# A transformer block on one core: one load moved to another queue, six more filling products, and all engine orders replaced

## The chip, the cores and the metric

The kernel runs on one core of a Trainium2 chip. The core has five engines that work side by side and meet only through semaphores: PE (TensorE, matrix products into PSUM), DVE (VectorE), ACT (ScalarE), POOL (GpSimd) and SP (SyncE, which here only issues transfers). In the profile PEld is PE's loading of weights. Each engine executes its own instructions strictly in the order in which the program lists them. Transfers are issued on SP's or ACT's queue and carried out by 16 DMA engines. The metric is the device time of one execution in microseconds (us); less is better. Three runs of the kernel before took 280.1, 280.29 and 282.09 us, so the median is 280.29 us.

## The reference

The input x has 2048 rows (tokens) of 448 columns, in bf16. A vector c gives six rows of 448 values, which shift, scale and gate the two halves of the block:

```
mod = silu(c) @ w_mod            # sa, ca, ga, sb, cb, gb
h = layernorm(x) * (1 + ca) + sa
x = x + ga * attention(h)        # 16 heads of 28, causal, window of 256 tokens
h = layernorm(x) * (1 + cb) + sb
x = x + gb * gmlp(h)
```

The attention makes q, k and v with one matrix (448 x 1344), takes a softmax over the last 256 tokens, and ends with a 448 x 448 matrix. The gMLP makes z = gelu(h @ w_in) of 1792 columns. It splits z into z1 and z2 of 896 columns each, normalises z2, mixes it over all tokens with w_sp (2048 x 2048) plus a bias per token, and multiplies the result with z1. Last comes w_out (896 x 448). The output has the shape of x.

## The kernel before, in words

The tokens lie on 16 tiles of 128, in four blocks of four tiles. The function builds a list of operations first (`sc.add`, with the helpers `pe`, `dve`, `act`, `pool`, `turn`, `load`). Each operation knows what it needs, which engines could execute it, and which buffers it takes. Nothing is planned in the program itself: `order()` reads the text `PLAN` at the top of the file. A word of it is a letter for the engine (p PE, a ACT, d DVE, t POOL, s SP), the number of the operation in the order of its creation, and, behind dots, the buffers it gets. The order of the words of one letter is the order of that engine's instructions. So `PLAN` sets three things: on which engine an operation runs, in which order each engine works, and which buffer (a PSUM bank, for instance) each operation gets. `waits()` then puts in the semaphore waits.

The work goes through these stages.

- **Head.** x's first block arrives in two pairs of tiles (`load_x0`, L410), w_mod's first part (`wmodA`) and the weights of k and q (`wq_st`, L406) in two halves each, one half on SP's queue and one on ACT's. After that SP loads the rest of x, the weights of v, and the rest of w_mod. DVE takes the statistics of x's tiles (L631, L634), POOL the reciprocal root (L638), DVE writes the normalised tile (`xn`, L649). PE computes the modulation from c (L548), transposes the tiles (L745), and ACT or DVE writes the modulated transposed tile (`hT`, L754 and L756). The weights of k and q are copied into a padded layout (`WQK`, L620 on DVE or POOL, L621 on ACT), in four pieces each. Then come the products for the keys (L826) and the queries (L802) of the first block.
- **Filling products.** `warm(n, ...)` (L567 to L571) adds n products of a constant with itself (L514), whose result nobody reads: 27 before the modulation's products and 4 behind them.
- **Attention.** For each of the 16 tiles there are score products (L931 for the first two tiles, L961 and L972 for the others), exponentials on ACT (L917, into `PW` and `PT`), masks on DVE (L980, L1001), and products with v (L1008). DVE divides by the sum (`rec_all` L1022, `o_sb` L1024), SP transposes the result (L467), PE multiplies with the output matrix (L1034), and DVE adds it to x (L1038). Between these, the projections of the later blocks (L768, L826, L846) are evacuated from PSUM on ACT (L777, L838, L850) or DVE (L778, L839, L851).
- **Second norm and gMLP.** Statistics, normalised tile and a transpose on SP again (L467, one for each tile), modulation (L1059, L1057), then products with w_in (L1128 for z2, L1149 for z1), gelu on ACT (L1135, L1157), and the normalisation of z2 (L1140).
- **Spatial products.** 28 groups of 16 products (L1173) mix z2 over the tokens. Their right operand is w_sp transposed, which SP brings from memory with transposing transfers: 16 for the first half (`wspA`), 16 for the second (`wspB`). The very first spatial group needs all normalised z2 and all 16 wspA. DVE adds the bias (L1177), POOL multiplies with z1 (L1180).
- **Output.** Groups of products with w_out (L1192), a sum with x on DVE (`fin`, L1202, four buffers), and a store on SP (L1207).

The order of the first loads on the two queues is written in the program too, as a constraint on the planner:

```
    for row in (t_x0[:1] + t_wmA[1:] + t_x0[1:] + t_wk[1:] + t_wq[1:], [t_c] + t_wmA[:1] + t_wk[:1] + t_wq[:1]):
        for first, then in zip(row, row[1:]):
            then.after = [first]
```

The first row is SP's queue: x's first pair, w_mod's second half, x's second pair, w_k's second half, w_q's second half. The second is ACT's: c, w_mod's first half, w_k's first half, w_q's first half.

Of the kernel before, what the change touches and what calls it, by code (L numbers as in the profile page):

```python
# [12 lines left out]
d22 p44.0 s2 t25 s4 a1 p45.0 p46.0 p47.0 p48.0 p49.0 s9 s6 s8 s11 t0 d103 p50.0 p51.0 p52.0 p35.0 t26 t27 a3  # L13
p53.0 p54.0 p55.0 p56.0 d104 p57.0 p58.0 p59.0 p60.0 p61.0 p62.0 p63.0 p64.0 t30 p65.0 p66.0 p67.0 t31 t28 a5
t29 s10 a7 a36 d21 a37 d101 d102 t105 t106 p68.0 p69.0 p70.0 t32 d108.0 d107.1 p40.0 p41.1 p42 d75 t93 p43 d94
p117.2 d76 d109 p71.1 p72.1 p73.1 t96 d111 a118 p74.1 p120.3 a121 p132.1 s12 d97 a119 d112 t95 a99 d110 t113
t114 d122 p133 a134 p141.3 p142 d100 a143 d98 p129.2 p130 a131 d115.0 d116.1 p123.1 a124 p138.0 d171 d173 d169
d175 d174 d172 p365.0 a366.0 d176 d170 t177 t178 p126.6 d127 t33 p139 p135.7 p136 d125 d128 p166.6 d179.0 s14
t23 s186 p156.1 d140 t34 d240 d184 p371.0 d236 a372.1 d182 p150.0 p157 t180 t181.1 d367 d234 s187 d235 p167
d241 d168 a158 p390.0 a391.2 a392 p147.1 p148 t185.2 s189 d373 p151 p144.6 p145 p397.0 t183.3 d237 d137 d149  # L20
p153.7 p163.1 a398.3 a399 d77 d152 t78 d369 p164 p79.0 d146 a165 s188 p80 d39 a162 p418.0 a419.4.0 t191 d238
d82 p83.1 p84 d375 d239 d81 p86.0 p87 p368.0 p370 d159 d400 p374 p376 d193 d192 p426.0 d85 p154 a190 p194.1
p195 d88 a427.1 p197.0 p198 p446.0 a196 t242 d402 s13 p210.1 p211 d299 s839 t243 a199 t247 d393 d244.0 d245
t24 d377 d378.0 p203.0 p204 a447.0.1 p394.0 p454.0 a205 d395 p396 p401 t249 d428 s19 p200.0 d305 s15 d212 a155
d423 p201 d429 p403 d202 a455.5 t250.1 a160 p225.1 p226 a227 p474.0 a475.3.2 p213.0 p214 p216.1 s17 d422 d161
d456 d404 d405.1 p420.0 a421 t246.2 t91 p217 d215 p424.0 p482.0 d218 p425 d301 a38 d208 d207 p222.0 p223 d206
a483.2 d451 p430 t248.3 p431 d432 d209 a224 p231.1 p232 a233 p448.0 a449 p501.0 p219.0 d450 a502.1.0 d90 s251
d433.2 p228.1 s252 s254 p229 p220 p452.0 p476.0 s253 d221 t255 p453 p458 s841 s18 a256 d457 d484 a477 a230
t258 p509.0 t257 a510.0 p259.0 d303 p260 p459 p268.1 s843 a261 d506 p269 p503.0 s406 p529.0 p265.0 p266 d478
d300 a504 a530.5.1 p531.0 d270 p275.1 p276 d304 t92 d306 d479 p537.0 a267 d460 d302 t307 a532 t308 a538.4 d505  # L30
d461.1 d309.0 s379 s462 d310 p262.0 p480.0 t311.1 p481 d485 p263 a264 d277 p281.1 d534 p486 p487 d511 d533
a271 p557.0 s316 p282 t312 a558.2.2 p278.0 p279 d488 s434 d489.0 s490 p507.0 p508 p513 a280 d539 p565.0 p290.0
p291 d512 p514 d273 d283 t314 d315.2 d540 d515 d516.2 s319 t89 p407.1 p408 a566.1 p559.0 p585.0 p535.0 p536
p541 d292 s317 a560 t313.3 p380.0 p381 d562 d409 d410 a586.0.0 p542 p593.0 d382 d561 p435.1 p436 p463.0 p464
d383 d437 a272 a274 p587.0 p284.1 a594.4 p285 d589 p612.0 d384 t385 a588 a286 p614.0 s517 d543 d544.0 p563.0
p287.1 p288 p564 a613.5.1 d567 p569 p620.0 a289 d465 p491.0 p492 s318 d595 t321 d568 a615 p570 p293.1 p294
d616 t323 a621.2 d493 p640.0 p518.0 p519 a295 d571 d596 t322 d572.2 d590 p591.0 a641.1.2 d520 s20 d320 d438
s545 d494 d439 p642.0 t386 p546.1 p547 p592 a643 p648.0 p597 p598 t440 t441 p330.0 d548 p670.0 d549 d495
p327.1 p328 p331 d387.0 a649.0 a329 d622 d599 d600.0 p668.0 s846 a669.4.0 p340.1 d332 p341 a342 d411 t412 t413
s573 p324.0 p325 a326 t414 p618.0 d617 p619 p624 p676.0 a677.5 t388 d442 d651 d623 p625 d466 d550 p346.1 p347  # L40
d672 a348 p333.0 p334 t443.1 p696.0 d467 d626 p574.1 d627.2 p575 d673 d551 a335 a697.2.1 t444 d645 s445 t415.2
t416 p352.0 p353 a354 d644 p646.0 s417 t468 t469 t470 p704.0 a705.3 d337 d650 p647 p652 d521 s601 d576 p349.0
p350 a671 s628 a351 d338 p296.1 p653 p297 p723.0 d700 p343.0 p344 d471.1 a298 s389 p355.1 d496 d678 d654 d336
d655.0 p674.0 d339 p675 a724.0.2 p698.0 p731.0 d679 t472 s473 p356 d706 t497 a345 a699 p602.0 p603 p680 d727
p725.0 p681 d577 a357 p358.1 p359 t814 a732.4 d707 d522 p751.0 t552 s656 d701 d682 d683.2 d604 d733 t523
p702.0 p703 s16 s684 a360 t524 d817 p629.0 a752.5.0 d734 p630 d631 s844 d498.2 t499 d578 p708 p709 d710 d711.0
p759.0 p657.1 d728 s845 d756 d579 p361.0 d755 a726 p658 a760.3 s712 p753.0 p729.0 p362 d762 p779.0 t553 p730
p735 a754 p736 a363 p781.0 d761 p685.0 p686 a780.2.1 d737 d738.2 p787.0 d659 d783 p757.0 p758 d784 p763 p764
d765 d766.0 p713.1 p714 d715 t815 a788.4 d789 d790 s500 t816 p863.0 p864.1 d687 p865 d688 a782 p785.0 p786
p791 p792 s739 t580 d660 t581 t525 t526.1 t527 s528 p740.1 d793 d794.2 p741 p866 p881.2 a867 d742 p882.3 p883  # L50
p884 d605 d606 t582.0 t583 a885 p1007.0 p1008.2 p1009 a892 t554.2 a874 t555 t607 t608 d661 s556 s584 d818
p1010 t821 t820 d819 p917.3 p918.1 p919 p920 t662 t663 d689 s767 a1011 a1013 a1014 p899.2 a921 s364 d869
p768.0 p769 d743 d744 t745 a1012 d609.0 d610 a928 d632 d633 t634 s795 p796.1 p797 p900.0 p901 p1015.1 p902
d664 d716 d717 s611 a903 d665.2 t635 p1016.2 p1017 p1018 d690 d636 a910 d886 t718 a1022 d666 t691 t692 t719
t693.1 t694 s834 d894 d770 d771 d772 d798 s667 d799 p1023.3 p1024.0 p1025 d875 s695 t637.0 p1026 t638 d876
d877 s639 s857 d868 d870 d800 d801 t746 t747 a1021 a1020 t748.2 d749 t802 t803 d887 a822 d893 s750 d720.1 t721
d825 t804.0 d888 t824 s832 a1019 d823 p935.2 p936.1 p937 p938 a1029 d773 t805 a1030 d912 d930 a1027 s722 d923
a1028 a939 t774 s806 p1039.0 p1040.3 p1041 t775 p953.2 a946 p954.1 p955 a1043 t878 t879 d889 t890 d922 d895
d905 d776.2 d777 s778 t896 d924 t871 t872 a827 d929 d931 a1044 d904 d941 s838 p956 p1042 s836 d947 a964 a957
t897 a1046 d940 t925 t926 d932 t811 t828 a1045 d948 t829 d826 p1031.0 d891 p971.1 p972.2 p973 p974 d949 p989.3  # L60
a975 d911 p990.1 p991 p992 a982 a993 p1032.2 a1000 d873 d913 p1047.3 p1033 p1034 a1037 d942 p1048.1 p1049
# [191 lines left out]
def bass_adaLN_cond__sliding_block__mixer_gmlp__prompt_kernel(  # L253
# [143 lines left out]
    t_c = load("d_c", "act", 0.01, lambda e: e.dma_start(c_row[127:128, :], c[0:1, :]), prio=-98.97, land=2.5)  # L397
# [15 lines left out]
    t_x0 = [load_x0(0, "sp", -98.99, 3.55)]  # L413
# [861 lines left out]
```

## Time and profile before

| what | value |
|---|---|
| median of three runs | 280.29 us (280.1 to 282.09) |
| time of the profiled execution | 282.43 us |
| its span, first to last instruction | 280.3 us |
| PE busy | 267.8 us (96%) |
| DVE busy | 166.6 us (59%) |
| ACT busy | 124.0 us (44%) |
| POOL busy | 124.5 us (44%) |
| instructions | 8415 |

The shares are means over stages of different kinds: ACT has no work after the first 160 us, and before that it is nearly full in the attention. Rows of the timeline have the start in us, the time in us, the engine, the line of the program, the operation, what it writes and from what, and how many instructions were merged; in brackets stands the idle time before the first of them and what ended it. A queue's own rows (SPq, ACTq) show how long the issue took, not when the data landed. Rows of groups have the shape, the count, busy us and mean ns of one, then the idle time before them.

### The profile page before, as it was taken

What the parts mean: (1) busy time and instruction counts of PE and PEld (TensorE: products, weight loads), DVE (VectorE), ACT (ScalarE), POOL (GpSimd) and SP (SyncE); (2) the same over time, 40 slices, a digit from 0 to 9 for tenths busy, and PEclk for the clock granted to TensorE, in tenths of its full rate; (3) what the DMA queues carried; (4) which work ended last, traced back from release to release, by engine and by line L of the source; (5) the groups of instructions that cost most, each with busy time, mean ns of one, the idle gap of its engine ahead of it and who ended that gap; (6) DMA issues with size and microseconds to landing.
All of it is one profiled execution on the core that took longest, in us unless ns stands there. A gap on an engine that the chain in (4) does not pass through costs nothing.

```text
span 280.3 us, 8415 instructions
## 1 busy us (share of the span) xinstructions
PE 267.8 (96%) x3736; PEld 154.3 (55%) x3746; DVE 166.6 (59%) x378; ACT 124.0 (44%) x144; POOL 124.5 (44%) x179
## 2 busy tenths in 40 slices
PE   7799988999999998999999699999999999999995
PEld 5777666676777675544444244444444545444452
DVE  3789899899899899959999301100300502224143
ACT  3479998989988997375876500000000000000000
POOL 7473445360646558383956203611454621036320
PEclk9899999999999999999999999999999999999999
DMA  7997798155604655485699999100000000100013
GB/s 217 302 228 114 176 110 170 22 61 86 103 5 60 124 115 81 95 190 77 138 146 173 181 191 194 16 0 0 0 2 0 6 2 27 49 0 2 0 66 115
DMA packets 66821, 25.54 MB, mean 91 GB/s; under 512 B 58465, under 2 KB 65698, under 8 KB 66786
## 3 DMA queue, kind: packets, MB, share of 16 engines
q1 hardware_dynamic: 66064, 24.21, 46.1%
q10 hardware_dynamic: 722, 0.80, 1.0%
q8 instruction: 29, 0.48, 0.8%
q14 instruction: 6, 0.05, 0.1%
HBM read 9.01 MB, written 1.84 MB: 39 GB/s over the span
## 4 chain that ended last, share of the span: by engine, by line
PE 74%; DVE 12%; ACT 6%; DMA 3%; issue 2%; POOL 1%; SPq 0%; DVEq 0%
PE ps L1173 34%; PE ps L1128 8%; PE ps L1149 8%; PE ps L1192 6%; ACT PW L917 5%; DVE PT L980 5%; PE ps L1008 4%; PE ps L1034 3%; DMA wq_st<-in_A_wqkv_dram 3%; PE ps L961 3%; PE ps L826 2%; PE ps L768 2%; PE ps L802 2%; PE ps L846 2%; DVE o_sb L1024 2%
## 5 line engine op out<-in xcount | busy, mean ns | idle before, releaser
L1180 POOL TENSOR_TENSOR z1T<-tmpg,z1T 128x512 bf16<-128x512 bf16 x28 | 31.9, 1154 | 75.9 <-DVE tmpg L1177 75.8
L917 ACT ACTIVATE PW<-ps 128x2048 bf16<-128x2048 f32 (+1 forms) x42 | 60.0, 1451 | 5.5 <-PE ps L961 4.0
L1177 DVE TENSOR_TENSOR tmpg<-ps,bsp_bc 128x512 bf16<-128x512 f32 x28 | 19.0, 689 | 72.8 <-PE ps L1173 67.3
L1173 PE MATMUL ps<-wspA,z 128*128 128x512 bf16 x220 | 48.9, 379 | 2.5 <-issue 2.3
L1173 PE MATMUL ps<-wspB,z 128*128 128x512 bf16 x218 | 49.2, 379 | 0.3
L980 DVE TENSOR_TENSOR PT<-PW,mask 128x1024 bf16<-128x1024 bf16 x56 | 38.9, 718 | 0.6 <-ACT PW L917 0.4
L1173 PEld LDWEIGHTS ps<-wspA,z 128*128 128x128 bf16 x224 | 21.8, 98 | 28.7 <-issue 2.6
L1173 PEld LDWEIGHTS ps<-wspB,z 128*128 128x128 bf16 x224 | 21.9, 98 | 26.1
L638 POOL TENSOR_TENSOR rs_all<-ve_all,neghalf 128x1 f32<-128x1 f32 (+2 forms) x37 | 25.0, 684 | 6.4 <-DVE xn L661 3.9
L1008 PE MATMUL ps<-Vaug,PT 128*128 128x32 bf16 x496 | 24.1, 177 | 2.1 <-DVE o_sb L1024 1.2
L1008 PEld LDWEIGHTS ps<-Vaug,PT 128*128 128x128 bf16 x496 | 21.8, 96 | 5.6 <-DVE o_sb L1024 2.0
L636 POOL TENSOR_SCALAR ve_all<-mv_all 128x1 f32<-128x1 f32 (+2 forms) x25 | 7.3, 294 | 35.3 <-DVE mv_all L634 31.6
L1128 PE MATMUL ps<-w_in,hT 64*128 64x448 bf16 x224 | 22.5, 349 | 0.0
L1192 PE MATMUL ps<-w_out_g,z1T 128*128 128x448 bf16 (+2 forms) x119 | 22.2, 341 | 0.0
L1149 PE MATMUL ps<-hT,w_in 64*128 64x512 bf16 x196 | 22.1, 376 | 0.0
L1202 DVE TENSOR_TENSOR fin<-ps,x_sb 128x448 bf16<-128x448 f32 (+2 forms) x17 | 9.6, 590 | 20.2 <-PE ps L1192 17.3
L631 DVE BATCH_NORM_STATS2 st_all<-x_sb 128x6 f32<-128x448 bf16 x32 | 19.3, 618 | 2.9 <-DMA x_sb<-in_A_x_dram 2.7
L1008 PE MATMUL ps<-Vaug,PW 128*128 128x32 bf16 x224 | 20.4, 176 | 0.5 <-issue 0.4
L826 PE MATMUL ps<-hT,WQK 112*128 112x128 bf16 x256 | 18.1, 223 | 1.9 <-POOL WQK L620 1.1
L631 DVE BATCH_NORM_STATS2 st_all<-z 128x6 f32<-128x448 bf16 x32 | 18.7, 608 | 1.0 <-ACT z L1135 0.9
L1135 ACT ACTIVATE z<-ps 128x896 bf16<-128x896 f32 x16 | 14.0, 916 | 11.5 <-PE ps L1128 9.0
L1008 PEld LDWEIGHTS ps<-Vaug,PW 128*128 128x128 bf16 x224 | 17.6, 96 | 1.8 <-issue 0.5
(106 smaller groups left out, 370.1 us busy)
## 6 DMA issues: line engine op xcount, KB each, us to landing
out_dram<-fin SPq DMA_DIRECT2D x15, 112.0 KB, 1.7
wmodB<-in_w_mod_dram SPq DMA_DIRECT2D x1, 1568.0 KB, 15.2
x_sb<-in_A_x_dram SPq DMA_DIRECT2D x3, 448.0 KB, 8.4
w_in<-in_B_w_in_dram SPq DMA_DIRECT2D x3, 448.0 KB, 4.7
w_out_g<-in_B_w_out_dram SPq DMA_DIRECT2D x1, 784.0 KB, 5.3
bsp_bc<-in_B_b_sp_dram SPq DMA_DIRECT2D x1, 512.0 KB, 5.7
x_sb<-in_A_x_dram SPq DMA_DIRECT2D x2, 224.0 KB, 4.6
hT<-xn SPq DMA_TRANSPOSE x28, 3.0
```

Source lines behind the costliest of these rows:

```text
L631: st = [dve(0.62 if True else 0, lambda e, t=t, ci=ci, s=s: e.bn_stats(st_all[:, slot, t, ci, :], s()), deps(t), prio) for ci, s in enumer ...
L638: return pool(0.4 + 0.15 * len(tiles), lambda e: e.tensor_tensor(rs_all[:, slot, a:b], ve_all[:, slot, a:b], neghalf[:, 0:b - a], ALU.pow) ...
L826: km = lambda g, kc, start, stop, h=h, t=t: lambda e: e.matmul(ps[:, h.slot[0], g * 128:(g + 1) * 128], lhsT=WQK[0:CP, kc, 16 + 4 * g:20 + ...
L917: ex = act(xdur, lambda e, out_ap=out_ap, in_ap=in_ap: e.activation(out_ap(), in_ap(), ACT.Exp, scale=SCALE), [s] + list(after), v - 8.0 + ...
L980: return lock_d(0.68, lambda e: e.tensor_tensor(cols(hp.slot[0] * 2048 + 1024 * k, [[256, 4], [128, 2], [1, 128]]), cols(at_w() + pad + at ...
L1008: fns.append(lambda e, hp=hp, hO=hO, hi=hi, bi=bi, kb=kb, hd=hd, nb=nb, a=at[hi][bi], p_of=p_of: e.matmul(ps[:, hO.slot[0], 32 * hd:32 * h ...
L1128: return lambda e, kc, p0, start, stop: e.matmul(ps[:, hs[t % 2].slot[hf], 0:D], lhsT=hT[p0:p0 + 64, kc, t * 128:(t + 1) * 128], rhs=w_in[ ...
L1149: return lambda e, kc, p0, start, stop: e.matmul(ps[:, hs[b // 2].slot[b % 2], :], lhsT=w_in[p0:p0 + 64, kc, ft * 128:(ft + 1) * 128], rhs ...
L1173: m = pe(16 * MMS, [lambda e, h=h, si=si, ft=ft, tb=tb: e.matmul(ps[:, h.slot[0], :], lhsT=z2[:, si, ft * 128:(ft + 1) * 128], rhs=(wspA i ...
L1177: a = dve(0.7, lambda e, h=h, ht=ht, tb=tb: e.tensor_tensor(tmpg[:, ht.slot[0], :], ps[:, h.slot[0], :], bsp_bc[:, tb * 512:(tb + 1) * 512 ...
L1180: u = pool(1.16, lambda e, ht=ht, ft=ft, tb=tb: e.tensor_tensor(z1T[tb][:, ft, :], tmpg[:, ht.slot[0], :], z1T[tb][:, ft, :], ALU.mult), [ ...
L1192: return [lambda e, ft=ft: e.matmul(ps[:, h.slot[0], 0:hi - lo], lhsT=z1T[t // 4][:, ft, (t % 4) * 128:(t % 4 + 1) * 128], rhs=w_out_g[:, ...
```

## The change

Three things are changed in the program. x's second pair of tiles is issued on ACT's queue, between ACT's halves of w_k and w_q, and no longer on SP's queue between w_mod and w_k. The second run of filling products has 10 and no longer 4. And the whole text `PLAN` is another one.

```
--- before.py
+++ after.py
 PLAN = """
-d22 p44.0 s2 t25 s4 a1 p45.0 p46.0 p47.0 p48.0 p49.0 s9 s6 s8 s11 t0 d103 p50.0 p51.0 p52.0 p35.0 t26 t27 a3
...
-t29 s10 a7 a36 d21 a37 d101 d102 t105 t106 p68.0 p69.0 p70.0 t32 d108.0 d107.1 p40.0 p41.1 p42 d75 t93 p43 d94
-p117.2 d76 d109 p71.1 p72.1 p73.1 t96 d111 a118 p74.1 p120.3 a121 p132.1 s12 d97 a119 d112 t95 a99 d110 t113
-t114 d122 p133 a134 p141.3 p142 d100 a143 d98 p129.2 p130 a131 d115.0 d116.1 p123.1 a124 p138.0 d171 d173 d169
...
+t25 a1 a3 a5 a9 s2 d22 t26 d21 s4 d109 s6 p44.0 p45.0 p46.0 p47.0 d110 p48.0 p49.0 p50.0 p51.0 t27 t30 p52.0
...
+p66.0 p67.0 p68.0 p69.0 p70.0 d107 d108 a36 d111 t112 d113.0 d114.1 p40.0 t100 p41.1 p42 p43 d81 d82 p123.2
+s10 d117 d115 a124 t23 p126.3 d99 d116 a127 d118 t101 t102 a125 t119 t120 a128 d103 a104 d106 d105 d121.0
+d122.1 t24 d181 p71.2 d175 p72.2 p73.2 p74.2 p75.2 a37 p76.2 p77.2 p78.2 p79.2 d179 p80.2 d177 t32 t34 p138.2
...
-    t_x0.append(load_x0(1, "sp", -98.97, 5.0))
-    for row in (t_x0[:1] + t_wmA[1:] + t_x0[1:] + t_wk[1:] + t_wq[1:], [t_c] + t_wmA[:1] + t_wk[:1] + t_wq[:1]):
+    t_x0.append(load_x0(1, "act", -98.85, 8.2))
+    for row in (t_x0[:1] + t_wmA[1:] + t_wk[1:] + t_wq[1:], [t_c] + t_wmA[:1] + t_wk[:1] + t_x0[1:] + t_wq[:1]):
...
-    warm(4, 0.12, -59.0)
+    warm(10, 0.12, -59.0)
```

The six added products have the numbers 75 to 80, so every operation from 75 on in the old list has a number greater by 6 in the new one: old 93 and new 99 are the same copy of a quarter of w_k. In the new head d117 and d115 are the statistics of x's tiles 3 and 2, d99 is that copy (on POOL in the old list: t93), d103, d106 and d105 are copies of quarters of w_q, d121 and d122 the normalised tiles 2 and 3.

The instructions of the engines are counted by the letters: PE 393 words before and 399 after, ACT 145 and 153 (one of the eight more is the load), DVE 378 and 383, POOL 175 and 163, SP 111 and 110. Ninety operations other than that load change their engine: 30 go from POOL to DVE, 21 from DVE to POOL, 16 from ACT to DVE, 20 from DVE to ACT, 3 from POOL to ACT.

SP's words from the second norm's transpose of tile 13 up to the last wspA, where hT stands for such a transpose with its tile, A for a wspA, B for a wspB and "bias" for the load of the spatial bias:

```
before: s750 hT13, s832 A, s722 hT12, s806 hT15, s778 hT14, s838 A, s836 A, s848 B, s835 A, s840 A, s837 A, s842 A, s830 bias, s852 B, s831 A, s833 A
after:  s756 hT13, s854 B, s784 hT14, s812 hT15, s840 A, s857 B, s842 A, s868 B, s844 A, s838 A, s849 A, s836 bias, s858 B, s841 A, s837 A, s843 A
```

The sets of products are the same apart from the fillers. The last spatial group is followed by seven output groups in the old list and by eight in the new one.

120 lines of the change are left out of this document (60 added, 60 removed).

## The prediction

> **What bounds the kernel now.** I read the page for the whole, the busy times by stretch of 20 us for the stages, the chain in order of time for the waits, and the timeline at the three places where the chain leaves TensorE. Page first, then the stretches (us, then busy us and instructions of PE, PEld, DVE, ACT and POOL, then clock, DMA share and GB/s):
> ```profile
> span 280.3 us, 8415 instructions
> ...
> PE 74%; DVE 12%; ACT 6%; DMA 3%; issue 2%; POOL 1%; SPq 0%; DVEq 0%
> ```
> ```profile
> 20.00:40.00 20.00, 19.51 (x503) 13.73 (x502) 18.74 (x45) 19.10 (x21) 8.75 (x12) 1.00 0.80 135
> 40.00:60.00 20.00, 18.56 (x553) 13.84 (x541) 18.60 (x37) 18.06 (x20) 10.99 (x11) 1.00 0.53 93
> 60.00:80.00 20.00, 19.73 (x579) 14.15 (x577) 18.74 (x39) 18.14 (x17) 6.59 (x8) 1.00 0.48 74
> 80.00:100.00 20.00, 19.86 (x607) 14.78 (x606) 18.85 (x43) 17.98 (x21) 10.88 (x17) 1.00 0.41 73
> 180.00:200.00 20.00, 19.89 (x92) 9.07 (x93) 2.92 (x5) 0.00 (x0) 4.85 (x5) 1.00 0.00 0
> ```
> The reader is to see two regimes. From 180 us on only PE has work, so no order of the same products can shorten it. In the attention, 20 to 100, DVE is busy 74.9 of 80 us and ACT 73.3: two engines close to full take turns as the limit, with 5.1 and 6.7 us of idle time between them and a gain. The rest of what can move is the head and one hole, which the chain and SP's timeline show:
> ```profile
> 148.72 8.20 PE ps L1149 x76
> 156.92 2.31 issue
> ```
> ```profile
> 137.18 2.64 SPq L467 DMA_TRANSPOSE wspA<-in_B_w_sp_dram  x2
> 139.86 3.12 SPq L467 DMA_TRANSPOSE wspB<-in_B_w_sp_dram  x1
> 143.02 5.61 SPq L467 DMA_TRANSPOSE wspA<-in_B_w_sp_dram  x4
> 148.69 0.56 SPq L1081 DMA_DIRECT2D bsp_bc<-in_B_b_sp_dram  x1
> 149.30 1.16 SPq L467 DMA_TRANSPOSE wspB<-in_B_w_sp_dram  x1
> 150.50 5.04 SPq L467 DMA_TRANSPOSE wspA<-in_B_w_sp_dram  x2
> ```
> ```profile
> DMA to landing us min/median/max: 3.2/4.0/7.2
> ```
> PE has finished the mixer's first products at 156.92 and does nothing for 2.31 us. The last two wspA transposes are issued between 150.50 and 155.54; the last row gives wspA's time from issue to landing, 4.0 at the median. The last issue begins about 1.3 us before 155.54, at 154.2, so it lands around 158.2, between 157.4 and 161.4. The spatial products (L1173) start at 159.23, which lies inside. So the hole is the wait for SP's last wspA.
>
> The head, in the timeline, and wq_st's own rows on ACT's queue (second line: issue to landing):
> ```profile
> 8.27 1.15 DVE L631 BATCH_NORM_STATS2 st_all<-x_sb 128x6 f32<-128x448 bf16 x2 [0.21 <-DMA x_sb<-in_A_x_dram]
> 9.32 0.62 PE L826 MATMUL ps<-hT,WQK 112*128 112x128 bf16 x8 [0.66 <-ACT hT L754]
> 9.83 1.07 POOL L620 COPY WQK<-wq_st 112x448 bf16<-112x448 bf16 x2 [1.42 <-DMA wq_st<-in_A_wqkv_dram]
> 10.54 0.58 ACT L621 ACTIVATE WQK<-wq_st 112x448 bf16<-112x448 bf16 x1 [0.81 <-DMA wq_st<-in_A_wqkv_dram]
> 10.99 2.11 PE L826 MATMUL ps<-hT,WQK 112*128 112x128 bf16 x24 [1.05 <-POOL WQK L620]
> 15.92 1.28 ACT L917 ACT_TABLE_LOAD   x1
> 17.22 1.02 ACT L917 ACTIVATE PT<-ps 128x1024 bf16<-128x1024 f32 x1
> ```
> ```profile
> L406 ACTq DMA_DIRECT2D wq_st<-in_A_wqkv_dram x2: 472/476/480, 1.8 to 2.3; - x2
> ...
> DMA to landing us min/median/max: 5.9/6.6/7.3
> ```
> Landings: ACT's half of w_k at 1.8 + 5.9 = 7.7, x's second pair at 8.27 (DVE starts on it), ACT's half of w_q at 2.3 + 7.3 = 9.6, SP's half of w_k at 9.83 (POOL starts), SP's half of w_q at 10.54. PE's first key products start at 9.32, and their second half waits 1.05 us for SP's half of w_k. The first exponential starts at 17.22. Clock by stretches of 3.4 us:
> ```profile
> 4.90:8.30 3.40, 3.05 (x53) 2.65 (x51) 1.54 (x8) 0.82 (x2) 1.83 (x4) 1.00 1.10 288
> 8.30:11.70 3.40, 1.69 (x27) 1.41 (x25) 2.52 (x8) 2.02 (x5) 1.90 (x5) 1.00 1.12 298
> 11.70:15.10 3.40, 3.40 (x36) 3.40 (x34) 3.00 (x10) 1.38 (x3) 0.36 (x1) 0.50 1.10 305
> ```
> PE is busy 1.69 of 3.40 us, and in the next 3.40 us it is granted half its clock, which costs up to 1.7 us of products there.
>
> **The change, part by part.**
>
> *Queues.* SP issues its half of w_k one place earlier. Two queues share 298 GB/s, 149 each, so 196 KB (0.20 MB) take about 1.35 us. SP's half of w_k would land near 8.2 instead of 9.8, and its half of w_q near 9.5. x's 224 KB now follow ACT's half of w_k, 7.7: at 149 GB/s they land at 9.2, at the pace of ACT's next 196 KB (9.6 - 7.7 = 1.9 us) at 9.9; I take 9.5, 1.2 us later than now. ACT's half of w_q comes behind them: 10.9 to 11.4, I take 11.1. The extra issue on ACT costs some 0.48 us there, before 4 us, while the modulation's products wait for w_mod until 6.5: hidden.
>
> [...]
>
> *DVE's order in the head.* The new list has d117 d115 (statistics of x's tiles 3 and 2) ahead of d99, a quarter of w_k's copy that was on POOL at 7.7. DVE runs in order, so this copy waits for x: 9.5 + 1.15 + 0.28 = 10.95, and the first key products start there, not at 9.32. SP's half of w_k is ready by then, so both halves run through, about 0.45 us each at full clock, to 11.9 instead of 11.4. Next now come the queries' products, with w_q copied at 11.1 + 0.3 (d103) and two more copies behind, 12.0; before, they started at 12.90, behind another key block. Then:
> - full clock: queries to 12.9, half a block and the second transposes to 13.6, scores near 14.1; ACT's evacuations to 15.1, table load 1.28, first exponential 16.4: 0.8 us earlier;
> - half clock until 15.1: queries to 13.8, scores near 15.8, first exponential 17.7: 0.5 us later.
>
> *Fillers.* Four took 0.43 us between PE's transposes, so ten take 1.1 us, from about 8.2 to 9.3, where PE now idles (0.66 us before 9.32). They delay nothing before 9.3. With the products from 10.95 on, PE is busy about 1.1 + 0.75 = 1.85 of the 3.40 us after 8.30, against 1.69 now: hardly more, because the wait for x gives back what the fillers add. The rows leave the threshold between 1.69 and 3.05. I take it that the clock still halves more often than not, but later products suffer less: head -0.2, bounds -0.8 and +0.5.
>
> [...]
>
> *Attention.* Seen from the lists, 12 instructions leave POOL (175 to 163), ACT gains 8 and DVE 5. Prices:
> ```profile
> L838 ACT ACTIVATE KT<-ps 128x512 bf16<-128x512 f32 x11 | 6.6, 597 | 1.8 <-PE ps L826 1.8
> L850 ACT ACTIVATE Vaug<-ps 128x448 bf16<-128x448 f32 x10 | 5.3, 547 | 1.0 <-PE ps L846 0.9
> L777 ACT ACTIVATE qT<-ps 128x512 bf16<-128x512 f32 x9 | 5.3, 600 | 0.2 <-PE ps L768 0.2
> L851 DVE CAST Vaug<-ps 128x448 bf16<-128x448 f32 x6 | 3.6, 603 | 0.0
> L839 DVE CAST KT<-ps 128x512 bf16<-128x512 f32 x5 | 3.4, 680 | 0.0
> L778 DVE CAST qT<-ps 128x512 bf16<-128x512 f32 x3 | 2.1, 689 | 1.6 <-PE ps L768 1.6
> L735 ACT ACTIVATE hT<-hT,modT 112x512 bf16<-112x512 bf16 x2 | 1.6, 818 | 0.0
> ```
> Between the first and the last exponential ACT gets 3 more V, 2 more K, 1 more modulation and 2 fewer Q: 1.64 + 1.19 + 0.82 - 1.20 = +2.45 us. Between the first mask and the last o_sb DVE loses 4 V, 2 K and, net, gains one Q: -2.41 - 1.36 + 0.69 = -3.1; the small pieces it takes from POOL and the fourteenth residual sum that now falls in this stretch put back some 1.2: -1.9. If DVE sets the pace, the stage is 1.9 shorter; if ACT does, 2.45 longer. Both carry the chain in turn, so I take the middle: +0.3. POOL has room (8.75 of 20 us busy).
>
> *SP before the spatial products.* After the last transpose of the second norm's result the old list has 8 wspA, 2 wspB and the bias load ahead of the last wspA, the new one 8 wspA and 3 wspB. One transpose costs 5.61 / 4 = 1.40 us of the queue. Upper bound +1.4. Against it, the new list sends tile 12's transpose before tile 13's, and counted from tile 13's both have 15 transposes left; POOL also has one norm less there (about 0.9 us), which may bring tile 13 forward: lower bound -0.9. I take half a transpose, +0.7. PE's work up to there is the same set, so it can't fill the longer hole.
>
> *Spatial products and tail.*
> ```profile
> 267.64 9.43 PE L1192 MATMUL ps<-w_out_g,z1T 128*128 128x448 bf16 x49
> ...
> 276.16 1.69 DVE L1202 TENSOR_TENSOR fin<-ps,x_sb 128x448 bf16<-128x448 f32 x3 [1.80 <-DMA out_dram<-fin]
> ```
> Seven output groups (49 products) follow the last spatial group now, eight then; their multiplication on POOL is covered in both lists, and the last sum waits for PE or for a free buffer within some 0.3 us: 0, bounds -0.3 and +0.3.
>
> *Sum.* -0.2 + 0.3 + 0.7 + 0 = +0.8 us. The profiled execution took 282.43 us (280.3 span and 2.1 around it), so it would become 283.2; the median shown, 280.29, becomes **281.1**.
>
> **The rivals.** *Faster:* the clock stays full (-0.8), DVE's relief goes through (-1.9), the tail saves 0.3: -3.0, 277.3. For it speaks that the chain names DVE twice as often as ACT; against it, that 1.85 of 3.40 us is nearly the 1.69 that lost the clock. Chance 0.12.
> *Slower:* ACT becomes the bound of the attention. Its extra 2.45 us turn into time as soon as in-order waits keep its 6.7 us of idle time between 20 and 100 us as they are; with the hole's 0.7 that is +3.2, 283.5, and with the outer bounds 284.9. For it speaks ACT's share, 92%, with exponentials that no other engine can take; against it, DVE's shorter turns. Chance 0.24.
> *The head's change doesn't do what it says:* x lands late, the copy behind its statistics holds the keys, the clock halves all the same: +0.5 in the head, 281.8 in all. Chance 0.24.
> The forecast has 0.40.
>
> **How the numbers follow.** A per cent, 2.8 us, is about what a measurement of this kernel can tell from no change (the runs shown lie between 280.1 and 282.09). The forecast and the head's failure fall within it: 0.64 same; 0.24 slower; 0.12 faster. All low ends together give -0.8 - 1.9 - 0.9 - 0.3 = -3.9 (276.4), all high ones +0.5 + 2.45 + 1.4 + 0.3 = +4.65 (284.9). All low ends at once are unlikely, the high ones less so, since ACT's load and SP's count are both written in the lists; 277.6 to 284.6 holds about 8 in 10.
>
> **What would show each step.** Queues: DVE's statistics of the second pair starting near 9.5, POOL's copy of SP's half of w_k near 8.7. Copy behind the statistics: the first key products near 11. Fillers: the granted clock after 11.7, 1.00 or 0.50. First exponential: between 16.4 and 17.7. Attention: ACT's busy share from 20 to 100 us up by about 2 us, DVE's down. The hole before L1173: 3 us instead of 2.31, with wspA as the last to land. The prediction is wrong if the attention's last exponential moves by over 2 us, or if x lands before 8.7.

## The result, and the profile after

| | kernel before | kernel after |
|---|---|---|
| median in the comparison, us | 281.5 (279.9 to 283.73, 20 runs) | 279.13 (278.12 to 281.02, 20 runs) |
| ratio after to before | | 0.993, interval 0.9907 to 0.9952 |
| profiled execution: time, span | 282.43, 280.3 | 279.06, 277.3 |
| mean granted clock of it | 0.994 | 0.998 |

The change makes the kernel 0.7% faster, between 0.5 and 0.9%. The prediction had it 0.3% slower, so the sign is wrong. That the time, 279.13 us, lies inside the predicted 277.6 to 284.6 owes more to the width of that range, 7 us, than to the sum.

Three places show where the two profiled executions part. The timeline's rows of the first z2 products and of the first spatial products, of the kernel before:

```profile
110.51 1.69 PE L1128 MATMUL ps<-w_in,hT 64*128 64x448 bf16 x16
...
159.23 2.10 PE L1173 MATMUL ps<-wspA,z 128*128 128x512 bf16 x9 [2.31 <-issue]
```

and of the kernel after, with the first exponential ahead of them:

```profile
16.27 1.02 ACT L917 ACTIVATE PT<-ps 128x1024 bf16<-128x1024 f32 x1
...
108.69 2.26 PE L1128 MATMUL ps<-w_in,hT 64*128 64x448 bf16 x22
...
156.11 5.14 PE L1173 MATMUL ps<-wspA,z 128*128 128x512 bf16 x23 [1.02 <-DMA wspA<-in_B_w_sp_dram]
```

The differences of these starts are the stages:

| stage, us | before | after | difference |
|---|---|---|---|
| start to first exponential | 17.22 | 16.27 | -0.95 |
| to the first z2 product (the attention) | 93.29 | 92.42 | -0.87 |
| to the first spatial product (with the hole) | 48.72 | 47.42 | -1.30 |
| to the end of the span | 121.07 | 121.19 | +0.12 |
| time outside the span | 2.13 | 1.76 | -0.37 |

The page of the kernel after:

```profile
span 277.3 us, 8439 instructions
...
PE 268.1 (97%) x3752; PEld 154.1 (56%) x3752; DVE 163.8 (59%) x383; ACT 126.7 (46%) x151; POOL 117.2 (42%) x167
...
PE 68%; DVE 9%; ACT 7%; SPq 6%; DMA 5%; issue 2%; ACTq 0%; POOL 0%; DVEq 0%
```

Read the PE share first: 268.1 of 277.3 us. All that is left to win outside PE's own work is 9 us of idle time; before it was 12.5, a part of which is products that the trace of before lacks (it has 3736 of 3746).

The head of the kernel after, in the timeline (start, time, engine, line):

```profile
9.50 1.15 DVE L631 BATCH_NORM_STATS2 st_all<-x_sb 128x6 f32<-128x448 bf16 x2 [0.95 <-DMA x_sb<-in_A_x_dram]
10.57 0.26 DVE L620 COPY WQK<-wq_st 112x448 bf16<-112x448 bf16 x1
10.68 0.58 ACT L621 ACTIVATE WQK<-wq_st 112x448 bf16<-112x448 bf16 x1
10.93 1.05 PE L826 MATMUL ps<-hT,WQK 112*128 112x128 bf16 x16 [1.03 <-ACT hT L754]
11.82 1.50 PE L802 MATMUL ps<-hT,WQK 112*128 112x128 bf16 x24
```

and its clock by stretches of 3.4 us (length, then busy us of PE, PEld, DVE, ACT and POOL, then the granted clock):

```profile
8.30:11.70 3.40, 2.37 (x33) 2.03 (x32) 2.18 (x9) 2.95 (x6) 1.93 (x6) 1.00 1.12 307
11.70:15.10 3.40, 3.29 (x61) 2.91 (x58) 2.64 (x6) 2.76 (x6) 1.48 (x4) 1.00 1.10 307
```

x's second pair, the copy behind its statistics and the key and query products come where the prediction had them, and the clock is not halved there.

The attention by stretches of 20 us, same columns:

```profile
20.00:40.00 20.00, 18.98 (x492) 13.93 (x489) 18.45 (x48) 18.39 (x20) 8.67 (x11) 1.00 0.52 93
40.00:60.00 20.00, 19.63 (x556) 13.38 (x553) 17.93 (x37) 18.38 (x22) 10.97 (x11) 1.00 0.71 117
60.00:80.00 20.00, 19.43 (x572) 14.51 (x574) 19.46 (x41) 18.38 (x18) 3.40 (x5) 1.00 0.75 121
80.00:100.00 20.00, 19.42 (x604) 14.25 (x596) 18.68 (x44) 18.21 (x19) 13.98 (x24) 1.00 0.47 77
```

ACT is busy 73.36 us of these 80, as before (73.3), and DVE 74.52 (74.9). The shares tell nothing here; the groups do. Between the first and the last exponential, the evacuations of values and keys on ACT, and of values on DVE, in the kernel before:

```profile
L838 ACT ACTIVATE KT<-ps 128x512 bf16<-128x512 f32 x9 | 5.4, 596 | 0.4 <-PE ps L826 0.4
L850 ACT ACTIVATE Vaug<-ps 128x448 bf16<-128x448 f32 x10 | 5.3, 547 | 1.0 <-PE ps L846 0.9
...
L851 DVE CAST Vaug<-ps 128x448 bf16<-128x448 f32 x6 | 3.6, 603 | 0.0
```

and in the kernel after:

```profile
L850 ACT ACTIVATE Vaug<-ps 128x448 bf16<-128x448 f32 x13 | 7.2, 552 | 0.4 <-PE ps L846 0.2
L838 ACT ACTIVATE KT<-ps 128x512 bf16<-128x512 f32 x11 | 6.6, 596 | 1.1 <-PE ps L826 1.0
...
L851 DVE CAST Vaug<-ps 128x448 bf16<-128x448 f32 x3 | 1.8, 614 | 0.0
```

Over all groups ACT has 3.0 us more of work beside the exponentials (25.0 against 22.0) and DVE 3.0 us less beside the large masks of L980 (56.8 against 59.8). These are sums of single times, which overlap in part; the busy time of the same stretch rises by 1.4 us on ACT and falls by 1.3 on DVE. The load did move, and the stretch became shorter.

The hole in the kernel after, on SP's queue (start, time of the issues) and in the chain of waits:

```profile
140.44 3.98 SPq L467 DMA_TRANSPOSE wspA<-in_B_w_sp_dram  x3
144.88 0.32 SPq L1081 DMA_DIRECT2D bsp_bc<-in_B_b_sp_dram  x1
145.25 1.23 SPq L467 DMA_TRANSPOSE wspB<-in_B_w_sp_dram  x1
146.53 7.15 SPq L467 DMA_TRANSPOSE wspA<-in_B_w_sp_dram  x3
```

```profile
151.59 4.47 DMA wspA<-in_B_w_sp_dram
156.11 69.24 PE ps L1173 x320
```

The last wspA is still the last thing that the first spatial product waits for, but PE idles 1.0 us there and not 2.31.

### The profile page after: what moved, and what is told of

It reads as the page before. It is cut to its first block, busy times and chain, and to the rows that moved or that the text cites. A ratio compares the mean times of both kernels' runs of the same rounds, so it can differ in the third digit from the quotient of the medians.

```text
span 277.3 us, 8439 instructions
## 1 busy us (share of the span) xinstructions
PE 268.1 (97%) x3752; PEld 154.1 (56%) x3752; DVE 163.8 (59%) x383; ACT 126.7 (46%) x151; POOL 117.2 (42%) x167
## 4 chain that ended last, share of the span: by engine, by line
PE 68%; DVE 9%; ACT 7%; SPq 6%; DMA 5%; issue 2%; ACTq 0%; POOL 0%; DVEq 0%
PE ps L1173 35%; SPq L467 6%; PE ps L1192 6%; ACT PW L917 5%; PE ps L768 4%; PE ps L1128 4%; PE ps L961 4%; PE ps L1008 4%; PE ps L1034 3%; PE ps L826 3%; DMA x_sb<-in_A_x_dram 3%; DVE PT L980 3%; PE ps L846 2%; DVE st_all L631 2%; DMA wspA<-in_B_w_sp_dram 2%
## 5 line engine op out<-in xcount | busy, mean ns | idle before, releaser
L980 DVE TENSOR_TENSOR PT<-PW,mask 128x1024 bf16<-128x1024 bf16 x56 | 38.8, 721 | 0.0
L1173 PEld LDWEIGHTS ps<-wspA,z 128*128 128x128 bf16 x224 | 21.8, 98 | 27.4 <-DMA wspA<-in_B_w_sp_dram 1.5
L1008 PE MATMUL ps<-Vaug,PT 128*128 128x32 bf16 x496 | 23.5, 177 | 0.3 <-DVE o_sb L1024 0.3
L1149 PE MATMUL ps<-hT,w_in 64*128 64x512 bf16 x196 | 21.8, 376 | 0.0
L826 PE MATMUL ps<-hT,WQK 112*128 112x128 bf16 x256 | 17.6, 219 | 2.3 <-ACT hT L754 1.0
L961 PE MATMUL ps<-qT,KT 32*128 32x128 bf16 (+5 forms) x1344 | 17.3, 197 | 0.7
```

The lines of the kernel that those rows point to most:

```text
L826: km = lambda g, kc, start, stop, h=h, t=t: lambda e: e.matmul(ps[:, h.slot[0], g * 128:(g + 1) * 128], lhsT=WQK[0:CP, kc, 16 + 4 * g:20 + ...
L961: fm.append(lambda e, hm=hm, qi=qi, key=key, kn=kn, lo=lo, hi=hi, col=col, p0=p0, t=t, j=j: e.matmul(ps[p0:p0 + kn, hm.slot[t], col:col + ...
L980: return lock_d(0.68, lambda e: e.tensor_tensor(cols(hp.slot[0] * 2048 + 1024 * k, [[256, 4], [128, 2], [1, 128]]), cols(at_w() + pad + at ...
L1008: fns.append(lambda e, hp=hp, hO=hO, hi=hi, bi=bi, kb=kb, hd=hd, nb=nb, a=at[hi][bi], p_of=p_of: e.matmul(ps[:, hO.slot[0], 32 * hd:32 * h ...
L1149: return lambda e, kc, p0, start, stop: e.matmul(ps[:, hs[b // 2].slot[b % 2], :], lhsT=w_in[p0:p0 + 64, kc, ft * 128:(ft + 1) * 128], rhs ...
L1173: m = pe(16 * MMS, [lambda e, h=h, si=si, ft=ft, tb=tb: e.matmul(ps[:, h.slot[0], :], lhsT=z2[:, si, ft * 128:(ft + 1) * 128], rhs=(wspA i ...
```

## The experiments

Fifteen kernels ran, in four rounds of three or four; one of them is the kernel after once more. Each stands beside runs of the kernel before in its own round, and the ratios are to these. For some readings only those executions are compared in which PE's mean granted clock was above 0.997, called *full clock* here. In every profile below that value the clock is halved for a stretch at least once; where slices of 1 us or less show its ends it lasts about 3.4 us (0.50 from 11.7 to 15.1 in the kernel before). No profile above that value has one while PE works.

### Where x's second pair is issued

The place alone, in the old kernel and taken back in the new one:

```
b_x_on_act (in before)      -load_x0(1, "sp", ...)   +load_x0(1, "act", ...)   PLAN: -s9   +a9 behind a5
a_x_on_sp  (in after)       -load_x0(1, "act", ...)  +load_x0(1, "sp", ...)    PLAN: -a9   +s9 behind s4
(cut: the two rows that fix the order of the first loads change with it)
```

> The kernel before with the second pair of x's tiles on ScalarE's queue behind half of w_k, and nothing else. By the walk of the prediction x lands 1.2 us later (9.5), the statistics and the copy of w_k follow, and key products start 0.5 to 1 us later: 280.5 to 281.5 us against 280.5 for the kernel before. If the place of x is what shortens the kernel after, it gives 279.2 to 280.

> The changed kernel with x's second pair of tiles back on SP's queue, between w_mod's half and w_k's half; all else as changed. My theory, that the new queue place buys nothing and that the new orders do: the statistics start near 8.3 us and no longer 9.5, the key products' first half near 10.1 and their second near 11.0 (SP's half of w_k lands near 9.8 again), the first exponential within 0.5 us of 16.3, and the time within 0.5 us of the changed kernel's, 2.0 to 2.4 us under the kernel before. The rival, that the queue place is what brings the head's gain: the first exponential is back near 17.2 and the time 0.8 to 1 us above the changed kernel's.

The old kernel with the new place: 281.32 us against 280.73, ratio 1.0014 (0.9988 to 1.0041). The new kernel with the old place: 278.91 us, ratio 0.9931 (0.9905 to 0.9957), the kernel after's own ratio. So the queue is no part of the gain. In the profiles with the new orders and ten fillers it costs the head a little: the first exponential starts at 16.27 with x on ACT's queue and at 15.88 with x on SP's.

### Fillers and the clock

```
a_4_fillers  (in after)   -warm(10, 0.12, -59.0)  +warm(4, 0.12, -59.0)   PLAN: the six words taken out
b_10_fillers (in before)  -warm(4, 0.12, -59.0)   +warm(10, 0.12, -59.0)  PLAN: the six words behind p126
```

> The changed kernel with four filling products behind the modulation, not ten. If the six fillers keep the clock: the granted clock falls to 0.50 for one stretch of 3.4 us near 12 to 15 us in some executions, the first exponential comes 0.5 to 1.4 us later there, and the median rises by 0.3 to 1 us. The rival, that PE's denser key and query products keep the clock and the fillers do nothing: the clock stays full and the time is within 0.3 us of the changed kernel's.

> The kernel before with the six more fillers alone, put behind the second transpose, where PE waits for hT. If the fillers keep the clock: full clock after 11.7 us, the products up to the first scores about 1.5 us shorter, first exponential up to 1 us earlier than 17.2, time 0.5 to 1 us under the kernel before. [...]

279.11 us, ratio 0.9948 (0.9916 to 0.998), and 280.21 us, ratio 0.9979 (0.9953 to 1.0006). Without the six fillers the median of the kernel after does not rise (279.13 with them, in another round; by the ratios it is 0.5 us more, with intervals that overlap), and the five executions of it at full clock have a median of 278.69. With the fillers the kernel before gains nothing that stands clear of noise. What can differ is how often the clock halves:

| kernel | executions below full clock |
|---|---|
| before, all four rounds | 25 of 106 |
| before with ten fillers; the same with the bias moved (below) | 2 of 12; 3 of 12 |
| after, first comparison and again | 0 of 20 and 4 of 10 |
| after with four fillers | 7 of 12 |

With the new orders and ten fillers 4 of 30 executions halve, and 5 of 64 when its variants `a_x_on_sp`, `a_bias_last`, `a_copy_first` and `a_x_sp_bias_last`, all with ten, are counted too, against 7 of 12 with four fillers. But the same kernel gave 0 of 20 and 4 of 10 in two rounds, so the share differs between rounds as well. With the old orders 5 of 24 is not told from 25 of 106. Executions with a granted clock of 0.992 to 0.994, which one halved stretch gives in the profiles of before, `after_again` and `b_10_bias_last`, take 0.8 to 1.6 us more than those at full clock in the kernel before, by the medians of the four rounds, and 1.6 in the kernel after (281.06 against 279.42, round of `after_again`). A quarter of the executions times 0.8 to 1.6 us is 0.2 to 0.4 us of the mean: the clock explains no more of the difference than that.

### The wait ahead of the spatial products

```
SP's words:  before        ... s842 A, s830 bias, s852 B, s831 A, s833 A
             b_bias_last   ... s842 A, s831 A, s833 A, s830 bias, s852 B
             after         ... s849 A, s836 bias, s858 B, s841 A, s837 A, s843 A
             a_bias_last   ... s849 A, s841 A, s837 A, s843 A, s836 bias, s858 B
```

> The kernel before with the load of the spatial bias and the third wspB issued behind the last wspA; nothing else moves. If the hole of 2.31 us before the first spatial product is SP's queue alone: the last wspA lands about 3 to 4 us earlier, before PE is done at 156.9, the hole shrinks to less than 0.5 us, and the time falls by 1.8 to 2.3 us. The rival, that the normalised z2 or something else would end the hole nearly as late: a gain under 0.7 us.

> The kernel after with the bias row and the sixth spatial weight group issued on SP's queue behind the last group of the other spatial weight. If the queue of SP sets the stretch between the attention's last product and the first spatial product, it loses what the profile after shows there beyond the 0.4 us that is left when the weight is in time (1.51 us in the profile after, 0.43 with the same move in the kernel before): 278.1 +- 0.4 us against 279.1 for the kernel after. If the stretch varies from execution to execution with what the transposing transfers ahead of it cost, and is small in most, the move buys no more than 0.3 us: 278.8 to 279.3.

279.81 us, ratio 0.9961 (0.9938 to 0.9984), and 278.39 us, ratio 0.9911 (0.9882 to 0.994). At full clock the move is worth 0.8 us in the old kernel (279.64 against 280.46 in the same round). In the new one it is worth about 0.6 us by the ratios (0.9911 against 0.993 and 0.9937 of the kernel after), in different rounds and with intervals that overlap. The chain of the old kernel with the move goes from the mixer's products to the spatial ones without a wait:

```profile
147.93 8.20 PE ps L1149 x76
156.13 3.99 PE ps L1173 x18
```

In the old kernel the wait was thus real, and set by SP's queue. That the gain is 0.8 us and not the 1.8 to 2.3 that was expected has a reason in the profiles: the wait isn't a constant of the order. Without the move, PE's idle time ahead of the first spatial product was 2.31, 1.40 and 0.21 us in three profiles with the old list of SP (before, x on ACT's queue, ten fillers), and 1.02, 1.06, 1.70, 1.80 and 0.48 in five with the new list (after, `after_again`, `a_x_on_sp`, `a_copy_first`, `a_4_fillers`). In the new kernel the move leaves a wait:

```profile
149.94 4.53 PE ps L1149 x42
154.47 0.70 issue
155.17 4.91 PE ps L1173 x22
```

There the 16 DMA engines were busy for 0.06 of the time from 153.97 to 154.93. DVE was busy until 154.85, with the last normalisations of z2 (L1140) by its order in the kernel after, which the move leaves alone, and PE began to load the first weights of the spatial products at 154.93. So in the new orders, as these times have it, the rival, the normalised z2, ends the wait nearly as late as SP's queue, and only a part of the 1.02 us was the queue's.

### Which engine evacuates, and the order

```
b_evac_moved (in before)  the letters of 21 evacuations (L777/L778, L806 to L808, L838/L839, L850/L851) as in the new PLAN, places kept
a_evac_back  (in after)   the letters of the same 21 as in the old PLAN, places kept
```

> The kernel before with the 21 evacuations of queries, keys and values that the change puts on the other engine (ScalarE or VectorE) moved so, each at its old place in the order. If the change's gain in the attention (first exponential to last: 90.6 us before, 89.3 to 90.4 after) comes from which engine evacuates, this kernel has it: 279.2 +- 0.5 us, first to last exponential 89.0 to 89.8. If it comes from the order of TensorE's work, the time stays at 280.5 +- 0.5, and the stretch at 90.6 or longer, since each moved evacuation stands at a place that was chosen for another engine.

> The kernel after with those 21 evacuations back on the engines that they had before, each at its new place. If the choice of engine is the gain: 280.3 +- 0.5 us and 90.6 us from the first exponential to the last. If the order is: 279.1 to 279.6 and 89.3 to 90.4 us.

290.88 us, ratio 1.032 (1.0254 to 1.0385), and 297.66 us, ratio 1.0591 (1.0537 to 1.0645): neither expectation holds. (One of the six executions of the first took 1482.99 us; why, no run here tells. The other five took 287.68 to 291.64.) The row of the large exponentials shows why, first of the old kernel with moved evacuations, then of the new one with old ones (behind the second bar: ACT's idle time ahead of them):

```profile
L917 ACT ACTIVATE PW<-ps 128x2048 bf16<-128x2048 f32 (+1 forms) x42 | 60.4, 1452 | 11.8 <-PE ps L961 10.2
```

```profile
L917 ACT ACTIVATE PW<-ps 128x2048 bf16<-128x2048 f32 (+1 forms) x42 | 60.2, 1453 | 16.3 <-PE ps L961 15.6
```

In the kernel after ACT waits 4.5 us there. An evacuation at a place chosen for another engine holds up that engine's queue: in the last kernel DVE stands 10.1 us in all ahead of its evacuations of values (L851), waiting for PE's products, against 0.0 in the kernel after. Then PE waits for DVE (4.6 us ahead of L1034), and ACT for PE's scores. So these two say nothing on the balance of the engines, only that engine and place are one choice.

### Three microseconds more for one engine at a time

To price each engine's load in the attention at unchanged orders, work was doubled in the kernel before.

```
b_act_twice   values of tiles 2, 6, 7, 8, 9 evacuated on ACT twice (the first time into a spare place)   +2.7 us of ACT
b_dve_twice   values of tiles 0, 1, 4, 5, 10 evacuated on DVE twice                                      +3.0 us of DVE
b_pe_twice    value products of tiles 4, 6, 8, 10 made twice                                             +3.0 us of PE
```

> The kernel before with five evacuations of values on ScalarE done twice (tiles 2, 6, 7, 8 and 9, between 33 and 70 us; the first of each pair goes to a spare place): 5 x 0.55 = 2.7 us more work for ScalarE in the attention and nothing else. If ScalarE sets the pace, as the slower rival had it, the time rises by 2 to 2.7 us against the kernel before of this round; if its idle time (7.5 to 9 us between the first and the last exponential) takes the work up, by 0 to 0.7.

> The kernel before with five evacuations of values on VectorE done twice (tiles 0, 1, 4, 5 and 10): 5 x 0.6 = 3.0 us more work for VectorE in the attention. If VectorE sets the pace there, +2 to +3 us; if its 5 to 7 us of idle time take the work up, 0 to 0.7; if the two engines share the limit half and half, as the prediction took it, about +1.5 here and about +1.4 for the run with ScalarE's work doubled.

> The kernel before with the four value products of tiles 4, 6, 8 and 10 done twice: 16 products of 448 columns more for TensorE in the attention, 16 x 0.19 = 3.0 us. TensorE is idle for only 2.6 to 3.6 us between the first and the last exponential. If TensorE sets the pace of the attention, +2.5 to +3 us; if VectorE and ScalarE do, +0 to +1.

| kernel | ratio to before | full clock, us (before 280.73) | share that became time |
|---|---|---|---|
| b_act_twice | 1.0016 (0.9986 to 1.0047) | 281.13 | 0.40 of 2.7: 0.15 |
| b_dve_twice | 1.007 (1.0037 to 1.0103) | 282.39 | 1.66 of 3.0: 0.55 |
| b_pe_twice | 1.0039 (1.0014 to 1.0064) | 281.75 | 1.02 of 3.0: 0.34 |

By these middle values ACT's load is nearly free, a good half of DVE's becomes time, and a third of PE's. None of the three looks like the bound alone. The intervals of the ratios are wide, though: -0.4 to 1.3 us for ACT, 1.0 to 2.9 for DVE, 0.4 to 1.8 for PE. Half and half, as the prediction took it, was to give about 1.5 us for DVE, which it did, and about 1.4 for ACT, which lies just outside. These prices hold for work added at these places; POOL's load, which falls from 124.5 to 117.2 us, was not priced.

### The kernel after again, the copy first, and the best of both

```
after_again        the kernel after, unchanged
a_copy_first       PLAN: s10 d117 d115 ... d99   ->   s10 d99 d117 d115 ...
a_x_sp_bias_last   a_x_on_sp and a_bias_last together
b_10_bias_last     b_10_fillers and b_bias_last together
```

> The kernel after once more, to stand beside the three others of this round on one chip and to give a second profile: 279.1 +- 0.4 us. If TensorE's idle time between the first exponential and the sixth pair's second is a matter of the order, it is 0.7 to 1.4 us here too (2.3 to 2.8 in the kernels with the old orders whose clock stayed full); the wait ahead of the first spatial product may come out anywhere between 0.4 and 2 us.

> The kernel after with the copy of the first half of w_k ahead of the statistics of x's second pair on VectorE. By the prediction's walk the first key products start at 9.3 to 10 us and not at 10.9. If the key products' late start is what sets the first exponential, that comes 0.5 to 1 us sooner and the time is 278.2 to 278.6; if the statistics' chain or the second half of w_q sets it, the first exponential stays at 16.0 to 16.3 and the time at 279.1 +- 0.4.

> The kernel after with the second pair of x's tiles back on SP's queue and with the bias row and the sixth spatial weight group behind the last group of the other spatial weight. Each alone gave 278.9 and 278.4 us; if the two gains add, 278.1 +- 0.4 us, and less than the kernel after in the same round; if the 0.2 us of x's place was chance, 278.4 to 278.7.

> The kernel before with the six added filling products and with the bias row and the sixth spatial weight group moved back: all that was found beside the orders, in the old orders. If the orders of the attention bring nothing, it comes to 278.4 +- 0.4 us like the new orders with the same move; if TensorE's 1 to 1.5 us of idle time in the attention and the 0.4 us outside the span belong to the orders, it stays 1 to 1.6 us above that: 279.4 to 280.0 us, at full clock in nearly every run.

| kernel | median, us | ratio to before | full clock, us (before 281.18) |
|---|---|---|---|
| after_again | 279.77 | 0.9937 (0.9912 to 0.9962) | 279.42 |
| a_copy_first | 279.24 | 0.993 (0.9905 to 0.9954) | 279.01 |
| a_x_sp_bias_last | 278.0 | 0.9892 (0.9862 to 0.9923) | 278.00 |
| b_10_bias_last | 280.05 | 0.9956 (0.9938 to 0.9974) | 279.81 |

The copy ahead of the statistics does start the keys sooner, and the first exponential doesn't follow. The timeline of that kernel:

```profile
9.94 1.08 PE L826 MATMUL ps<-hT,WQK 112*128 112x128 bf16 x16 [0.27 <-ACT hT L754]
11.93 1.50 PE L802 MATMUL ps<-hT,WQK 112*128 112x128 bf16 x24 [0.91 <-DVE WQK L620]
16.36 1.02 ACT L917 ACTIVATE PT<-ps 128x1024 bf16<-128x1024 f32 x1
```

The queries wait for the last copy of w_q, so the late keys of the kernel after cost the first exponential nothing.

The new orders with x back on SP's queue and the bias behind the last wspA beat the kernel before by 1.1% (0.8 to 1.4%). They lie 1.4 us below the kernel after at full clock in the same round; these are six executions each, whose ranges overlap (277.46 to 279.61 and 278.6 to 280.01). In the chain of the new one the hole is 0.70 us:

```profile
147.98 6.04 PE ps L1149 x56
154.02 0.70 issue
154.72 5.34 PE ps L1173 x24
```

The old orders with all that was found beside the orders reach 279.81 at full clock (in 9 of 12 executions, where nearly all were expected), 1.8 us above that, and the intervals of the two ratios do not overlap. x's place, the number of fillers and the place of the bias are the same in both: this difference is that of the text `PLAN`, its engines, orders and buffers.

## Why the prediction was wrong

The step that failed is the attention's term. It was taken as +0.3 us, half for DVE's relief and half for ACT's load; the profiles at full clock show about -1.7. This alone turns the sign of the sum. The branch of the clock, the hole's +0.7 and the time outside the span were wrong too.

**Landings and copies of the head: right.** x at 9.50 (taken: 9.5), the copy behind the statistics done at 10.83 (10.95), the first key products at 10.93 (10.95), queries at 11.82, first exponential at 16.27 where the full-clock branch had 16.4. The move to the other queue brought no gain by itself (ratio 1.0014 in the old kernel; taken back in the new one, 0.9931 beside 0.993). The prediction's two signs of being wrong did not appear: x landed at 9.50, and the last exponential's start moved from 107.85 to 106.72.

**The clock: the wrong branch.** "The clock still halves more often than not" failed: 26 of 30 executions of the kernel after were at full clock. The estimate of PE's busy time behind it was low too, 2.37 of 3.40 us where it had 1.85. Nor is there one threshold between 1.69 and 3.05, which was an estimate from those rows: with four fillers and 1.61 of 3.40 the kernel after kept its clock (last section). The profiled execution of before was not typical in this: three quarters of that kernel's executions have full clock. In profiles of such ones with the old queue the first exponential starts at 15.41 to 15.45 (`b_act_twice`, `b_pe_twice`, `b_bias_last`) and at 16.10 (with ten fillers), not at 17.22. Beside these the new head is 0.2 to 0.9 us later; the -0.95 of the table above compares a head at half clock with one at full clock. For the two profiled executions the term -0.2 should have been -0.95, and at full clock +0.2 to +0.9.

**The attention: wrong sign.** The counts were right: 3 more values, 2 more keys and 2 fewer queries on ACT are in the groups. The term +0.3 came from taking the middle between -1.9 (DVE sets the pace) and +2.45 (ACT does). From the first exponential to the first z2 product, at full clock after the head, four profiles with the old orders have 93.29 to 94.27 us (mean 93.6) and six with the new ones 91.29 to 92.42 (mean 91.9): -1.7. An early first exponential goes with a long attention (15.45 with 94.27, 16.10 with 93.39), so the start of the first z2 product is the safer measure: 109.46 to 109.72 in the three of the old profiles whose head had full clock, 107.60 to 108.69 in the six new ones (108.69 in the kernel after itself), 1.5 us sooner in the mean.

The prices measured by the doubled work would have given 0.15 x 2.45 - 0.55 x 1.9 = -0.7. With the loads that the profiles show, 3.0 us more on ACT and 3.0 less on DVE, they give -1.2. So the half weight on ACT was one error, and the 1.2 us that DVE was to get back seems to be another. That taking work away gains what adding it costs is an assumption, and 0.5 to 1.0 us stay without a price. The page's chain named DVE 12% and ACT 6%, which pointed the right way, but it is no safe hint: with the same orders and ten fillers it names ACT 12% and DVE 6%.

PE's idle time shows where the gain lies. Up to the end of the last exponential PE idles 3.0 to 4.4 us in the four old profiles and 1.7 to 2.7 in the six new ones. Most of that is in one place: from 36 to 56 us PE idles 1.85 us with the old orders at full clock (ten fillers, first row) and 0.37 in the kernel after (second row); it is 1.7 to 2.0 in all four old profiles and 0.3 to 0.7 in all six new ones:

```profile
36.00:56.00 20.00, 18.15 (x512) 13.43 (x512) 18.35 (x37) 18.07 (x20) 8.63 (x9) 1.00 0.58 97
```

```profile
36.00:56.00 20.00, 19.63 (x528) 13.97 (x527) 18.11 (x37) 18.73 (x20) 9.40 (x8) 1.00 0.67 115
```

What PE waits for there in the kernel before is DVE (us in all, times, the longest):

```profile
PE ps L1008 <- DVE o_sb L1024: 1.2, 2, 0.8
```

Products with v stand behind DVE's division of an earlier tile (`o_sb`). Such a wait of 0.5 to 1.0 us near 46 us is in all four old profiles. In the kernel after PE's only wait named between 36 and 56 us is 0.25 us, for ACT's keys. So DVE's division came too late in the old orders and no longer does in the new ones. Whether that is DVE's smaller load or its new order, and which single move does it, stays open, since engine and place could not be changed apart.

PE's share of 96% belonged ahead of the shares of DVE and ACT: from the first exponential's start to the last one's, 90.6 us, PE idles 2.7 us in the kernel before, so with the same products there was little more than that to win.

**The hole: +0.7 did not come.** The extra wspB was to cost half a transpose. From the end of the last hT issue to the landing of the last wspA both profiled executions need the same 21.8 us: 137.14 to 158.93 before, 134.27 to 156.06 after. The stalls of SP's queue (7.15 us for three issues in the rows above, where three took 3.98 just before) are larger than one transpose and differ between executions. From the first z2 product to the first spatial one it is 46.67 to 48.72 us in the three profiles with the old list of SP and 46.89 to 48.19 in the four with the new one at full clock, with equal means within 0.1 us. The -1.30 of the table above thus belongs to the two profiled executions and not to the orders. (In both lists 7 wspA and the bias load stand between the last hT and the last wspA; the difference, one wspB, was read rightly.)

**Spatial products and tail: right**, +0.12 us with 0 taken.

**Outside the span: not in the sum.** Every execution with the old orders has 2.10 to 2.23 us around its span, every one with the new orders 1.67 to 1.80. These 0.4 us are a quarter of the gain at full clock. Why they go with the orders, no run here tells.

At full clock, then: head and attention together -1.5, hole and tail about 0, outside -0.4: -1.9, where the round of `after_again` measured 279.42 - 281.18 = -1.76. Of the rivals, the faster one, given 0.12, had the right sign for DVE's relief and the right branch of the clock, which is worth 0.4 us of the mean at most. The slower one, ACT as the bound, does not hold: it would have made 2 to 2.7 us of the doubled work on ACT, and 0.40 was measured (1.3 at the most).

## What to carry to other kernels

Before a balance between engines is read off their shares, look at the engine with the least idle time, and price the loads of the others by doubling a few evacuations in place: it takes one run an engine and gives a measured weight, with its interval, where a middle between two bounds is a guess. Check by the granted clock whether the profiled execution is a typical one before its stages are used as the base of a sum. Here 21 evacuations moved to another engine at their old places cost 3 to 6%; engine and place have to be chosen together.

## What was not expected of the hardware

Whether the clock halves differs between executions of one kernel (0 of 20 and 4 of 10 of the kernel after), and where it halves isn't confined to the head. In the second profile of the kernel after (`after_again`) it does so in the attention. By stretches of 1 us:

```profile
29.00:30.00 1.00, 0.93 (x8) 0.40 (x5) 1.00 (x4) 1.00 (x1) 0.78 (x1) 1.00 0.20 62
30.00:31.00 1.00, 0.00 (x0) 0.00 (x0) 1.00 (x4) 0.74 (x2) 0.26 (x1) 1.00 0.05 6
31.00:32.00 1.00, 0.53 (x10) 0.53 (x11) 1.00 (x4) 0.00 (x0) 0.28 (x1) 1.00 0.00 0
32.00:33.00 1.00, 1.00 (x55) 0.73 (x53) 0.80 (x2) 0.60 (x1) 0.92 (x2) 0.95 0.33 72
33.00:34.00 1.00, 1.00 (x4) 0.32 (x3) 0.00 (x0) 0.97 (x1) 1.00 (x1) 0.50 1.19 72
```

The first profile of the same kernel has the same stall, a little shorter, and keeps its clock:

```profile
30.00:31.00 1.00, 0.09 (x2) 0.00 (x0) 1.00 (x3) 0.95 (x2) 0.40 (x1) 1.00 0.00 0
31.00:32.00 1.00, 0.94 (x24) 0.84 (x28) 1.00 (x6) 0.06 (x1) 0.13 (x1) 1.00 0.00 0
```

PE idles 1.5 us in the one and 1.0 in the other, and behind the longer idle the clock falls, about 1.5 us after PE is back at work, for 3.4 us (from 32.95 to 36.3). The length of the stall doesn't decide it alone. In the profile of the kernel after with four fillers PE is idle for 1.79 us between 8.30 and 11.70, all of it ahead of its key products by the page (L826, 1.8 us for ACT's hT), and is busy for less of 3.40 us than the 1.69 after which the clock of the kernel before fell. Yet the clock stays full (length, PE, PEld, DVE, ACT, POOL, then the clock):

```profile
8.30:11.70 3.40, 1.61 (x27) 1.34 (x25) 2.21 (x10) 2.68 (x6) 1.74 (x5) 1.00 1.13 286
11.70:15.10 3.40, 3.29 (x60) 2.90 (x58) 2.46 (x7) 2.85 (x5) 1.60 (x5) 1.00 1.10 305
```

So the clock fell behind 1.5 us of idle time in one profile and stayed full behind 1.8 us in another. Nor was PE idle all the while ahead of a fall: it worked 1.69 us of the 3.40 ahead of the one in the kernel before, and 1.86 of the 3.40 in the second profile of the kernel after (29.55 to 32.95). What decides it, no run here shows.
